# A gated S5/FFN kernel on one core: the first two pairs of w1 tiles in halves of 256 tokens, and the first loads spread over three queues

## The chip, the cores and the metric

One core of a Trainium2 chip runs the whole program. The metric is device time in microseconds (us); lower is better. Three runs of the kernel before gave 141.84, 142.42 and 142.87 us, median 142.42. Engines are named as in the profile: PE (TensorE matmul), PEld (its weight loads), DVE (VectorE), ACT (ScalarE), POOL (GpSimd), SP (SyncE, which here only issues transfers).

## The reference

For `x` of 2048 tokens by 448 features (bf16) the kernel computes a gated mix of a state-space layer `a` and a feed-forward layer `b`:

```python
g = sigmoid((x * gate_w).sum(-1, keepdims=True))
# a: complex diagonal recurrence, 448 states
dt = exp(log_dt); Lam_bar = exp(dt * Lam)
B_bar = ((Lam_bar - 1.0) / Lam)[:, None] * Bmat      # Bmat = B_re + 1j*B_im
Bu = einsum("bld,pd->blp", x, B_bar)
h_t = Lam_bar * h_{t-1} + Bu_t
a = 2.0 * einsum("blp,dp->bld", h, Cmat).real + x * Dskip
# b: 448 -> 1792 -> 448
b = silu(x @ w1) @ w2
out = g * a + (1 - g) * b
```

## The kernel before

**Tiling.** Tokens are cut into four chunks of 512 (`CH`). `x` is loaded token-major into `xnat` and transposed on PE into `xT` (features on partitions, in four blocks of up to 128). Each product tile is 128 output rows by 512 tokens and contracts 448 features as seven steps of 64 rows; two tiles make a *pair*, whose steps run side by side, one in the upper and one in the lower 64 rows of the PE array (L670). A pair has two halves: h=0 with four steps, h=1 with three. "F" tiles are rows of `x @ w1` (14 per chunk), evicted by ACT with Silu into `aT` (L641); "B" tiles are `x @ B` (7 per chunk), evicted into `UG` (L647 on DVE for the first chunk, L649 on ACT later). Then come the second feed-forward product (L775), the state rotation and scans on DVE (L705, L737), and the read-out with C (L796, `ot` L799, stores L802).

**What sets the order.** Every operation is entered in a `Plan` with an estimated cost and a priority; `order()` lists them by estimated time. PE is in order: its instructions run as they were entered. Loads are operations of the queue that issues them (`load`, L387 to L390): SP, ACT or POOL, each in the order that the plan gives. `Waits` then puts in semaphore waits; a flag `own` on a PE operation makes it wait also for earlier PE results in the same PSUM bank.

**The start, where the change is.**

- Warm-up: `NWARM` = 6 matmuls of 128x512 and one of 256 columns on constants (L463, L464), then the transposes of the first chunk of `x` (`x0_transposes`, L478; evictions L486 on DVE and L488 on ACT), then two fill matmuls (L499).
- `x` of the first chunk comes in two halves of 256 tokens (224 KB each): the first on SP's queue, the second on ACT's, both as the first issue of their queue. All 32 transposes are done before the first product.
- `w1` is cut into column groups (`w1cuts`, L392): W0 to W3 of 256 columns each (two F tiles each, one pair), and W4 of 768 columns. Each group is issued as its first 384 rows (192 KB, W4: 576 KB) and its last 128 rows (64 KB, W4: 192 KB); W0 goes as 128 KB on SP and two pieces of 64 KB on ACT.
- SP's order: x (first half), W0 (128 KB), three parameter rows (0.9 KB each), W1, W2, W3, then matrix B in four pieces, then W4, two broadcast rows (`gwb`, `dkb`), the next chunk of x, w2, C, and the last two chunks of x. The pieces of B, called B1 to B4 below, are A_B_re rows 0 to 383 (B1, 336 KB), A_B_re's last 64 rows (B2, 56 KB), A_B_im's last 64 rows (B3, 56 KB) and A_B_im rows 0 to 383 (B4, 336 KB). They land in tile `H`.
- POOL starts with constants (L443 to L456; the last that matters here is `SG`, L454), then waits for the parameters: `prmT` transposes them on PE (L543), DVE copies them to `pc` (L547), POOL takes a power (`dtc`, L550), and from there DVE makes phase tables (L551 to L569) and ACT sines and cosines (L567, L570).
- `x_products` enters the products. Pair 0 is W0's two tiles, pair 1 W1's, pair 2 W2's, pair 3 W3's. Its PE order is: pair 0 h=0, prmT, pair 1 h=0, pair 0 h=1, pair 2 h=0, pair 1 h=1, pair 3 h=0, then the transposes of B1 (24, L611, evictions L619 and L621), pair 2 h=1, the transposes of B2 to B4 (32, L611), then the first pair of B tiles and so on. All of this is in one in-order list, so a late operand holds up everything behind it.

Of the kernel before, what the change touches and what calls it, by code (L numbers as in the profile page):

```python
# [17 lines left out]
CH = 512  # L18
# [2 lines left out]
NFB = F_FF // 128  # L21
NSLOT = 7
NOT = 5
NWARM = 6
NFILL = 2
XCOL = [0, 128, 256, 320]

# [4 lines left out]
PE_MM = {512: 0.2157, 448: 0.1891, 128: 0.0560}  # L32
# [244 lines left out]
def bass_gated_mix__ssm_conv_s5__dense_activation_silu__prompt_kernel(nc, A_x, A_Lambda_re, A_Lambda_im, A_B_re, A_B_im, A_C_re, A_C_im,  # L277
               A_log_dt, A_Dskip, B_x, B_w1, B_w2, gate_w, out):
    with ExitStack() as ctx:
# [6 lines left out]
        x2, out2 = A_x[0], out[0]  # L286

        xnat = sb("xnat", [128, NTB, D_MOD], BF16)
        xT = sb("xT", [128, 4, S_TOK], BF16)
# [24 lines left out]
        ident = sb("ident", [128, 128], BF16)  # L314
# [8 lines left out]
        prm = sb("prm", [3, 512], BF16)  # L323
# [8 lines left out]
        SG = sb("SG", [128, 2, 4], F32)  # L332
# [25 lines left out]
        def bk(t, k=0):  # L358
            return ps[:, t.bank + k, :]
# [7 lines left out]
        def act_cost(n, aps=0):  # L367
            return 0.17 + n * 0.000833 + 0.09 * aps
# [4 lines left out]
        def ACT(fn, r, w, cost, prio, tag=""):  # L373
            return P.add("act", fn, r, w, cost, prio, tag=tag)

        def DVE(fn, r, w, cost, prio, tag=""):
            return P.add("dve", fn, r, w, cost, prio, tag=tag)

        def POOL(fn, r, w, cost, prio=10, tag=""):
            return P.add("pool", fn, r, w, cost, prio, tag=tag)  # L380

        def PE(fn, r, w, cost, tag=""):
            return P.add("pe", fn, r, w, cost, 0, tag=tag)
# [3 lines left out]
        def load(q, dst, src, name, nbytes, prio=None, after=()):  # L387
            nl[0] += 1
            prio = nl[0] if prio is None else prio
            P.add(q, lambda e: e.dma_start(dst, src), list(after), name.split(), 0.6 if q == "pool" else 0.5, prio, sem(), nbytes, tag="ld " + name)  # L390
# [3 lines left out]
        def load_w1(q, k, a, b):  # L394

            cols = slice(w1cuts[k], w1cuts[k + 1])
            src = B_w1[320:448, cols] if a == 3 else B_w1[128 * a:128 * b, cols].rearrange("(b p) f -> p b f", p=128)
            load(q, w1s[:, 3, cols] if a == 3 else w1s[:, a:b, cols], src, " ".join(f"w1_{k}_{i}" for i in range(a, b)),
                 256 * (b - a) * (cols.stop - cols.start))

        for h, q in enumerate(("sp", "act")):
            load(q, xnat[:, 2 * h:2 * h + 2, :], x2[256 * h:256 * h + 256, :].rearrange("(b p) d -> p b d", p=128), f"xn0{h}", 256 * 896)
        load_w1("sp", 0, 0, 2)
        load_w1("act", 0, 2, 3)
        load_w1("act", 0, 3, 4)
        for k, v in enumerate((A_log_dt, A_Lambda_re, A_Lambda_im)):
            load("sp", prm[k:k + 1, 0:448], v.rearrange("(o n) -> o n", o=1), f"prm{k}", 896)
        for k in range(1, len(w1cuts) - 2):
            load_w1("sp", k, 0, 3)
            load_w1("sp", k, 3, 4)  # L410
        Bnat = H[3][:, :, 0:D_MOD]
        load("sp", Bnat[:, 0:3, :], A_B_re[0:384, :].rearrange("(b p) d -> p b d", p=128), "H3_0 H3_1 H3_2", 384 * 896)
        load("sp", Bnat[0:64, 3, :], A_B_re[384:448, :], "H3_3", 64 * 896)
        load("sp", Bnat[64:128, 3, :], A_B_im[384:448, :], "H3_3i", 64 * 896)
        load("sp", Bnat[:, 4:7, :], A_B_im[0:384, :].rearrange("(b p) d -> p b d", p=128), "H3_4 H3_5 H3_6", 384 * 896)
        btn = {s: [f"BT{s}_{h}" for h in range(2)] for s in range(7)}
        load_w1("sp", len(w1cuts) - 2, 0, 3)
        load_w1("sp", len(w1cuts) - 2, 3, 4)
# [35 lines left out]
        POOL(lambda e: e.tensor_single_scalar(SG[:, 1, 3:4], sgn[:, :], -1.0, ALU.mult), ["SG", "sgn"], ["SG"], 0.2, 2)  # L454
        POOL(lambda e: e.memset(hpi[:, :], HALFPI), [], ["hpi"], 0.1, 2)
        POOL(lambda e: e.memset(eul[:, :], math.e), [], ["eul"], 0.1, 0)  # L456
        ACT(lambda e: e.preload_act_table_set("silu_and_others"), [], ["tbl"], 1.3, 9.5)

        tkz = Ps()
# [8 lines left out]
        def x0_transposes(q0, part, who):  # L468

            tk = Ps(2)  # L470

            def mm(pe):
                for q in (q0, q0 + 1):
                    for k in range(2):
                        o = ((q - q0) * 2 + k) * 64
                        for h in range(2):
                            p = slice(64 * h, 64 * h + 64)
                            r = pe.transpose(bk(tk, h).bitcast(BF16)[:, o:o + 64], xnat[p, 2 * part + k, XCOL[q]:XCOL[q] + 128], ident[p, p])  # L478
                return r
            PE(mm, [f"xn0{part}", "ident"], [tk], 4 * 0.054, "xT0")  # L480
            for h in range(2):
                src = lambda h=h: bk(tk, h).bitcast(BF16)[:, 0:256].rearrange("p (q b n) -> p q b n", q=2, n=64)
                dst = xT[:, q0:q0 + 2, 256 * part:256 * part + 256].rearrange("p q (b h n) -> p q b h n", h=2, n=64)[:, :, :, h, :]
                names = [f"xT0_{q}{part}{h}" for q in (q0, q0 + 1)]
                if who[h] == "d":
                    DVE(lambda e, src=src, dst=dst: e.tensor_copy(dst, src()), [tk], names, 0.28, 0, "xTe")  # L486
                else:
                    ACT(lambda e, src=src, dst=dst: e.activation(dst, src(), AF.Copy), [tk], names, act_cost(256), 0, "xTe")  # L488

        x0_transposes(0, 0, "da")  # L490
        x0_transposes(0, 1, "da")
        x0_transposes(2, 0, "da")
        x0_transposes(2, 1, "dd")

        tkw = Ps()

# [3 lines left out]
            return r  # L500
        PE(fill, [], [tkw], NFILL * 0.11, "fill")
        xn_of = {tc: {q: [f"xT{tc}_{h}" for h in range(2)] for q in range(4)} for tc in range(1, NCH)}
        xn_of[0] = {q: [f"xT0_{q}{part}{h}" for part in range(2) for h in range(2)] for q in range(4)}

        def x_transposes(tc, who):

# [29 lines left out]
        def parameters():  # L536

            prmn = [f"prm{k}" for k in range(3)]
            tkp = Ps()

            def prm_t(pe):
                for b in range(4):
                    r = pe.matmul(bk(tkp)[:, 4 * b:4 * b + 3], prm[0:3, 128 * b:128 * b + 128], ident[0:3, 0:3], start=True, stop=True)  # L543
                return r
            DVE(lambda e: e.tensor_copy(prm[:, 448:512], prm[:, 384:448]), prmn + ["xT0_211"], ["prm4"], 0.17, 0)
            PE(prm_t, prmn + ["prm4", "ident"], [tkp], 0.5, "prmT")
            DVE(lambda e: e.tensor_copy(  # L547
                pc[:, 0:3, :], bk(tkp)[:, 0:16].rearrange("p (b k) -> p k b", k=4)[:, 0:3, :]), [tkp], ["pc"], 0.2, 0)
            LDT, LRE, LIM = (pc[:, k, :] for k in range(3))
# [73 lines left out]
        def w1n(fb, i):  # L623
            return [f"w1_{q}_{i}" for q in range(len(w1cuts) - 1) if w1cuts[q] <= fb * 128 < w1cuts[q + 1]]

        def weights(tile, p0, p1, i):
            kind, tc, k = tile
            return w1s[p0:p1, i, k * 128:k * 128 + 128] if kind == "F" else BT[p0:p1, i, LCOL[k]:LCOL[k] + 128]
# [25 lines left out]
        def x_products(tiles, fill={}, wait=()):  # L654

            part = (list(zip([(i, 64) for i in (0, 1, 2, 3)], [(i, 0) for i in (0, 1, 3, 2)])),  # L660
                    list(zip([(i, 0) for i in (0, 1, 2)], [(i, 64) for i in (0, 1, 3)])))
            pairs = [tiles[t:t + 2] for t in range(0, len(tiles), 2)]
            toks = [Ps(2) for _ in pairs]

            def steps(k, h, a, z):
                def body(pe):
                    for n, cut in list(enumerate(part[h]))[a:z]:
                        for b, ((i, p0), tile) in enumerate(zip(cut, pairs[k])):
                            tc = tile[1]
                            r = pe.matmul(bk(toks[k], b), weights(tile, p0, p0 + 64, i), xT[p0:p0 + 64, i, tc * CH:(tc + 1) * CH],  # L670
                                          start=(h == 0 and n == 0), stop=(h == 1 and n == 2))
                    return r
                reads = [n for cut in part[h][a:z] for (i, _), tile in zip(cut, pairs[k])
                         for n in xn_of[tile[1]][i] + (w1n(tile[2], i) if tile[0] == "F" else btn[tile[2]])]
                return PE(body, list(dict.fromkeys(reads)), [toks[k]], (z - a) * PE_MM[512], f"{pairs[k][0][0]}{pairs[k][0][1]}")

            def half(k, h):
                if h == 0 and pairs[k][0] == ("F", 0, 0):
                    steps(k, 0, 0, 2)
                    steps(k, 0, 2, 4)  # L680
                else:
                    steps(k, h, 0, len(part[h])).own = h == 1
                if h:
                    evict(pairs[k], toks[k])

            half(0, 0)
            for f in fill.get(-1, ()):
                f()
            for k in range(len(pairs)):
                order = [lambda: half(k, 1)] + [lambda: half(k + 1, 0)] * (k + 1 < len(pairs))  # L690
                for n, f in enumerate(order if k - 1 in wait else order[::-1]):
                    f()
                    for m in fill.get((k, n), ()):
                        m()
                for f in fill.get(k, ()):
                    f()
# [223 lines left out]
```

## Time and profile before

| what | value |
|---|---|
| median of three runs | 142.42 us (141.84 to 142.87) |
| the profiled execution's own time | 142.07 us |
| its span in the profile | 140.2 us |
| DVE busy | 123.2 us (88%) |
| ACT busy | 89.0 us (63%) |
| POOL busy | 38.7 us (28%) |

The profile shows one execution. "L670" is line 670 of the kernel. A group of instructions is given with its line, its engine, what it writes and reads (`out<-in`), its shape and how often it ran. The chain of waits that ended last lists, in order of time, start, length and the work that the end of the program hangs on. A timeline gives start, length, engine, line and, in brackets, how long the engine was idle before and what ended that; "<-issue" means that nothing that the profile shows did. SPq, ACTq and POOLq are issues of transfers: their length is the issue, not the transfer, and the time to landing stands in the list of DMA issues. A table by windows gives each engine's busy time and the busy share of the 16 DMA engines in a stretch.

### The profile page before, as it was taken

How to read it: one execution, taken by the hardware profiler on the slowest of the kernel's cores; microseconds unless marked ns; L12 is line 12 of the kernel's file. 1: busy time of each engine (PE TensorE's matmuls, PEld its weight loads, DVE VectorE, ACT ScalarE, POOL GpSimd, SP SyncE). 2: the span in 40 equal slices, each digit the busy share in tenths (PEclk: the TensorE clock that was granted, in tenths of full speed). 3: DMA queues.
4: the chain of work that ended last, by engine and by line, in shares of the span. 5: the costliest groups of instructions: out<-in, count | busy, mean ns of one | idle time of the engine just before them, and what ended most of it. 6: DMA issues, size and time to landing. Idle time of an engine off the chain costs nothing.

```text
span 140.2 us, 3002 instructions
## 1 busy us (share of the span) xinstructions
PE 136.7 (97%) x1199; PEld 67.5 (48%) x1199; DVE 123.2 (88%) x179; ACT 89.0 (63%) x155; POOL 38.7 (28%) x72
## 2 busy tenths in 40 slices
PE   7999999999999999999999999999999999999992
PEld 2445554445544544455554544444455555555561
DVE  0369999999999999999999999999699999599153
ACT  3239758999998998713971886899920068412300
POOL 7160004201545600229560002833000204222220
PEclk9999999999999999999999999999999999999999
DMA  4988999820447730108975000947001402245342
GB/s 142 262 254 251 320 380 271 201 55 0 69 78 123 126 45 0 37 0 127 158 142 139 0 5 0 134 92 115 2 2 57 106 0 37 33 98 120 46 94 70
DMA packets 18500, 14.71 MB, mean 105 GB/s; under 512 B 2867, under 2 KB 18358, under 8 KB 18486
## 3 DMA queue, kind: packets, MB, share of 16 engines
q0 software_dynamic: 6064, 5.51, 24.7%
q1 hardware_dynamic: 11862, 8.65, 20.4%
q10 hardware_dynamic: 560, 0.36, 0.8%
q8 instruction: 9, 0.15, 0.5%
q14 instruction: 5, 0.04, 0.1%
HBM read 7.17 MB, written 1.84 MB: 64 GB/s over the span
## 4 chain that ended last, share of the span: by engine, by line
PE 97%; DVE 0%; issue 0%
PE ps L670 46%; PE ps L775 31%; PE ps L796 15%; PE ps L463 2%; PE ps L515 1%; PE ps L478 1%; PE ps L815 1%; PE ps L611 1%; PE ps L499 0%; DVE ot L799 0%; PE ps L464 0%; PE ps L543 0%
## 5 line engine op out<-in xcount | busy, mean ns | idle before, releaser
L670 PE MATMUL ps<-xT,w1s 64*128 64x512 bf16 x392 | 48.6, 380 | 0.0
L775 PE MATMUL ps<-w2s,aT 128*128 128x448 bf16 x224 | 43.4, 353 | 0.0
L641 ACT ACTIVATE aT<-ps 128x1024 bf16<-128x1024 f32 (+1 forms) x30 | 28.7, 970 | 10.8 <-PE ps L670 10.6
L775 PEld LDWEIGHTS ps<-w2s,aT 128*128 128x128 bf16 x224 | 21.6, 98 | 20.7 <-issue 0.8
L670 PEld LDWEIGHTS ps<-xT,w1s 64*128 64x128 bf16 x392 | 20.0, 95 | 22.7 <-issue 1.2
L670 PE MATMUL ps<-xT,BT 64*128 64x512 bf16 x196 | 25.8, 376 | 0.0
L783 POOL DMA_DIRECT2D xnat<-fe x16 | 13.9, 889 | 38.1 <-ACT fe L781 35.7
L781 ACT ACTIVATE fe<-ps,g 128x448 bf16<-128x448 f32 x16 | 10.1, 633 | 21.8 <-PE ps L775 17.8
L390 POOL DMA_DIRECT2D UG<-Gf x27 | 15.1, 566 | 30.4 <-DVE Gf L737 30.0
L737 DVE TENSOR_TENSOR_SCAN Gf<-rc,gin,H 128x512 f32<-128x512 f32 x14 | 17.0, 1268 | 0.0
L796 PE MATMUL ps<-CP,H 128*128 128x448 bf16 (+2 forms) x98 | 16.4, 326 | 0.0
L670 PEld LDWEIGHTS ps<-xT,BT 64*128 64x128 bf16 x196 | 11.1, 94 | 10.8
L799 DVE SCALAR_TENSOR_TENSOR ot<-ps,g,xnat 128x448 bf16<-128x448 f32 (+2 forms) x18 | 10.8, 626 | 4.6 <-issue 3.3
L705 DVE TENSOR_TENSOR H<-UG,COS 128x3584 bf16<-128x3584 bf16 (+4 forms) x10 | 12.7, 1272 | 0.0
L796 PEld LDWEIGHTS ps<-CP,H 128*128 128x128 bf16 x98 | 8.9, 98 | 7.5 <-issue 0.4
L649 ACT ACTIVATE UG<-ps 128x1024 bf16<-128x1024 f32 (+1 forms) x12 | 10.7, 916 | 1.8 <-PE ps L670 1.8
L705 DVE TENSOR_TENSOR PO<-UG,SIN 128x1536 bf16<-128x1536 bf16 (+1 forms) x8 | 8.7, 1091 | 2.9 <-ACT UG L747 1.5
L390 POOL DMA_DIRECT2D UG<-UG x8 | 4.6, 580 | 23.0 <-ACT UG L649 11.6
L850 ACT ACTIVATE xnat<-xnat,g 128x448 bf16<-128x448 bf16 x16 | 10.0, 665 | 0.2
L843 ACT ACTIVATE junk<-xg 128x448 bf16<-128x448 bf16 x16 | 9.2, 573 | 0.2
L705 DVE TENSOR_TENSOR PI<-UG,SIN 128x512 bf16<-128x512 bf16 (+2 forms) x13 | 9.2, 730 | 0.0
L737 DVE TENSOR_TENSOR_SCAN Gf<-rc,gin,H2C 128x512 f32<-128x512 f32 x7 | 8.5, 1269 | 0.0
(102 smaller groups left out, 124.9 us busy)
## 6 DMA issues: line engine op xcount, KB each, us to landing
UG<-Gf POOLq DMA_DIRECT2D x21, 128.0 KB, 2.4
xnat<-fe POOLq DMA_DIRECT2D x16, 112.0 KB, 2.8
out_dram<-ot SPq DMA_DIRECT2D x15, 112.0 KB, 1.7
w2s<-in_B_w_dram SPq DMA_DIRECT2D x1, 1568.0 KB, 11.6
xnat<-in_A_x_dram SPq DMA_DIRECT2D x3, 448.0 KB, 7.6
w1s<-in_B_w_dram SPq DMA_DIRECT2D x4, 192.0 KB, 3.4
w1s<-in_B_w_dram SPq DMA_DIRECT2D x1, 576.0 KB, 6.4
UG<-UG POOLq DMA_DIRECT2D x8, 64.0 KB, 2.3
```

The lines of the kernel that those rows point to most:

```text
L390: P.add(q, lambda e: e.dma_start(dst, src), list(after), name.split(), 0.6 if q == "pool" else 0.5, prio, sem(), nbytes, tag="ld " + name)
L641: ACT(lambda e, src=src, dst=dst: e.activation(dst, src(), AF.Silu), [tk, "tbl"], [f"aT{tc % 2}_{m}" for m in names], act_cost(512 * n), 2 ...
L649: ACT(lambda e, src=src, dst=dst: e.activation(dst, src(), AF.Copy), [tk], [f"{un}{m}" for m in names], act_cost(512 * n), 5, "U")
L670: r = pe.matmul(bk(toks[k], b), weights(tile, p0, p0 + 64, i), xT[p0:p0 + 64, i, tc * CH:(tc + 1) * CH], start=(h == 0 and n == 0), stop=( ...
L705: DVE(lambda e: e.tensor_tensor(o, a, b, op), r, w, dve_cost(n, 2), prio, tag)
L737: DVE(lambda e, s=s, b=b, init=init: e.tensor_tensor_scan(Gf[:, s, :], rc[:, b:b + 1].to_broadcast([128, CH]), A[:, s, :], init, ALU.mult, ...
L775: r = pe.matmul(bk(tk)[:, 0:D_MOD], aT[tc % 2][:, fb, o:o + 128], w2s[:, fb, :], start=(fb == 0), stop=(fb == NFB - 1))
L781: ACT(lambda e: e.activation(f[:, :], bk(tk)[:, 0:D_MOD], AF.Copy, scale=g1[:, tb:tb + 1]), [tk, f"g1_{tc}"], [fn], act_cost(448, 1), 7, "fe")
L783: P.add("pool", lambda e: e.dma_start(Tb[:, tb, :], f[:, :], accum_op=ALU.add), [fn, f"Tb{tb}"], [f"Tb{tb}"], 0.94, 2, sem(), 115000, tag= ...
L796: r = pe.matmul(bk(tk)[:, 0:b - a], H[tc][:, s, o:o + 128], CP[:, s, a:b], start=(s == 0), stop=(s == NSLOT - 1))
L799: DVE(lambda e, tk=tk, a=a, b=b: e.scalar_tensor_tensor(ot[tb % NOT][:, a:b], bk(tk)[:, 0:b - a], g[:, tb:tb + 1], Tb[:, tb, a:b], ALU.mul ...
L850: ACT(lambda e, tb=tb: e.activation(Tb[:, tb, :], xnat[:, tb, :], AF.Copy, scale=g[:, tb:tb + 1]), [f"xd{tc}", f"g_{tc}"], [f"Tb{tb}"], ac ...
```

## The change

1. **Warm-up.** `NWARM` goes from 6 to 5.
2. **Queues.** SP issues x's first half, the three parameter rows, x's second half, W1, W2, W3, W4 and the rest as before. ACT issues all of W0 (128, 64 and 64 KB), no x. POOL issues B1 to B4, in this order, after `SG` (L454 before) and ahead of `dtc`.
3. **Transposes.** The 32 transposes of x's first chunk are split: 16 for its first half of tokens ahead of the first product, 16 for its second half after prmT. Their evictions are DVE and ACT in turn throughout; DVE's copy of the parameters comes ahead of the second two.
4. **Products.** Pairs 0 and 1 are done in halves of 256 tokens (`of`): 56 matmuls of 256 columns instead of 28 of 512. The new PE order up to pair 3 is: pair 0 h=0 (first tokens), prmT, transposes of the second tokens, pair 0 h=1 (first), pair 1 h=0 (first), pair 0 h=1 (second), pair 1 h=1 (first), pair 0 h=0 (second), pair 1 h=1 (second), pair 2 h=0 (all tokens), pair 1 h=0 (second), pair 3 h=0, transposes of B1, pair 2 h=1, transposes of B2 to B4. From pair 3 on nothing is reordered on PE.

```diff
-NWARM = 6
+NWARM = 5
...
-        for h, q in enumerate(("sp", "act")):
-            load(q, xnat[:, 2 * h:2 * h + 2, :], x2[256 * h:256 * h + 256, :].rearrange("(b p) d -> p b d", p=128), f"xn0{h}", 256 * 896)
-        load_w1("sp", 0, 0, 2)
+        def load_x0(h):
+            load("sp", xnat[:, 2 * h:2 * h + 2, :], x2[256 * h:256 * h + 256, :].rearrange("(b p) d -> p b d", p=128), f"xn0{h}", 256 * 896)
+
+        load_x0(0)
+        load_w1("act", 0, 0, 2)
         load_w1("act", 0, 2, 3)
         load_w1("act", 0, 3, 4)
         for k, v in enumerate((A_log_dt, A_Lambda_re, A_Lambda_im)):
             load("sp", prm[k:k + 1, 0:448], v.rearrange("(o n) -> o n", o=1), f"prm{k}", 896)
+        load_x0(1)
...
-        load("sp", Bnat[:, 0:3, :], A_B_re[0:384, :].rearrange("(b p) d -> p b d", p=128), "H3_0 H3_1 H3_2", 384 * 896)
-        load("sp", Bnat[0:64, 3, :], A_B_re[384:448, :], "H3_3", 64 * 896)
-        load("sp", Bnat[64:128, 3, :], A_B_im[384:448, :], "H3_3i", 64 * 896)
-        load("sp", Bnat[:, 4:7, :], A_B_im[0:384, :].rearrange("(b p) d -> p b d", p=128), "H3_4 H3_5 H3_6", 384 * 896)
...
+        load("pool", Bnat[:, 0:3, :], A_B_re[0:384, :].rearrange("(b p) d -> p b d", p=128), "H3_0 H3_1 H3_2", 384 * 896, -1, ["SG"])
+        load("pool", Bnat[0:64, 3, :], A_B_re[384:448, :], "H3_3", 64 * 896, -1, ["SG"])
+        load("pool", Bnat[64:128, 3, :], A_B_im[384:448, :], "H3_3i", 64 * 896, -1, ["SG"])
+        load("pool", Bnat[:, 4:7, :], A_B_im[0:384, :].rearrange("(b p) d -> p b d", p=128), "H3_4 H3_5 H3_6", 384 * 896, -1, ["SG"])
...
         x0_transposes(0, 0, "da")
-        x0_transposes(0, 1, "da")
         x0_transposes(2, 0, "da")
-        x0_transposes(2, 1, "dd")
...
-            DVE(lambda e: e.tensor_copy(prm[:, 448:512], prm[:, 384:448]), prmn + ["xT0_211"], ["prm4"], 0.17, 0)
-            PE(prm_t, prmn + ["prm4", "ident"], [tkp], 0.5, "prmT")
+            DVE(lambda e: e.tensor_copy(prm[:, 448:512], prm[:, 384:448]), prmn + ["xT0_200"], ["prm4"], 0.17, 0)
+            PE(prm_t, prmn + ["prm4", "ident"], [tkp], 0.27, "prmT")
...
-            def steps(k, h, a, z):
+            def steps(k, h, a, z, of=(0, 1)):
+                t0, t1 = 256 * of[0], 256 * of[-1] + 256
                 def body(pe):
                     for n, cut in list(enumerate(part[h]))[a:z]:
                         for b, ((i, p0), tile) in enumerate(zip(cut, pairs[k])):
-                            tc = tile[1]
-                            r = pe.matmul(bk(toks[k], b), weights(tile, p0, p0 + 64, i), xT[p0:p0 + 64, i, tc * CH:(tc + 1) * CH],
-                                          start=(h == 0 and n == 0), stop=(h == 1 and n == 2))
+                            o = tile[1] * CH
+                            r = pe.matmul(bk(toks[k], b)[:, t0:t1], weights(tile, p0, p0 + 64, i), xT[p0:p0 + 64, i, o + t0:o + t1],
+                                          start=(h == of[0] and n == 0),
+                                          stop=(h != of[0] and n == len(part[h]) - 1))
                     return r
...
+            def begin():
+                steps(0, 0, 0, 2, (0,))
+                steps(0, 0, 2, 4, (0,))
+                for f in fill.get(-1, ()):
+                    f()
+                x0_transposes(0, 1, "da")
+                x0_transposes(2, 1, "da")
+                steps(0, 1, 0, 3, (0,)).own = True
+                steps(1, 0, 0, 4, (0,))
+                steps(0, 1, 0, 3, (1,))
+                steps(1, 1, 0, 3, (0,)).own = True
+                steps(0, 0, 0, 4, (1,)).own = True
+                evict(pairs[0], toks[0])
+                steps(1, 1, 0, 3, (1,))
+                half(2, 0)
+                steps(1, 0, 0, 4, (1,)).own = True
+                evict(pairs[1], toks[1])
```

More of the change, by code (lines that the diff above doesn't have):

```diff
@@ L502, in bass_gated_mix__ssm_conv_s5__dense_activation_silu__prompt_kernel @@
         xn_of = {tc: {q: [f"xT{tc}_{h}" for h in range(2)] for q in range(4)} for tc in range(1, NCH)}
-        xn_of[0] = {q: [f"xT0_{q}{part}{h}" for part in range(2) for h in range(2)] for q in range(4)}
         def x_transposes(tc, who):
@@ L672, in body @@
                     return r
                 reads = [n for cut in part[h][a:z] for (i, _), tile in zip(cut, pairs[k])
-                         for n in xn_of[tile[1]][i] + (w1n(tile[2], i) if tile[0] == "F" else btn[tile[2]])]
-                return PE(body, list(dict.fromkeys(reads)), [toks[k]], (z - a) * PE_MM[512], f"{pairs[k][0][0]}{pairs[k][0][1]}")
+                         for n in ([f"xT0_{i}{t}{u}" for t in of for u in range(2)] if tile[1] == 0 else xn_of[tile[1]][i])
+                         + (w1n(tile[2], i) if tile[0] == "F" else btn[tile[2]])]
@@ L677, in half @@
+                return PE(body, list(dict.fromkeys(reads)), [toks[k]], (z - a) * PE_MM[512] * len(of) / 2, f"{pairs[k][0][0]}{pairs[k][0][1]}")
             def half(k, h):
[L678 to L682, printed above, removed]
+                steps(k, h, 0, len(part[h])).own = h == 1
                 if h:
                     evict(pairs[k], toks[k])
-            half(0, 0)
@@ L687, in x_products @@
-            for f in fill.get(-1, ()):
-                f()
-            for k in range(len(pairs)):
+            def begin():
[15 more added lines that the diff above has]
+                evict(pairs[1], toks[1])
@@ L690, in x_products @@
+            k0 = 0
+            if pairs[0][0] == ("F", 0, 0):
+                begin()
+                k0 = 2
+            else:
+                half(0, 0)
+            for k in range(k0, len(pairs)):
                 order = [lambda: half(k, 1)] + [lambda: half(k + 1, 0)] * (k + 1 < len(pairs))
```

## The prediction, made before the changed kernel ran

> **What bounds the kernel now.** I read the page's busy times first, then the chain of waits that ended last, then the timeline of the first 16 us with the DMA issues.
>
> ```profile
> PE 136.7 (97%) x1199; PEld 67.5 (48%) x1199; DVE 123.2 (88%) x179; ACT 89.0 (63%) x155; POOL 38.7 (28%) x72
> ```
>
> ```profile
> 0.76 2.72 PE ps L463 x6
> ...
> 3.70 1.12 PE ps L478 x29
> 4.82 0.54 PE ps L499 x2
> 5.36 1.59 PE ps L670 x7
> ...
> 7.13 3.99 PE ps L670 x36
> 11.13 0.35 PE ps L611 x24
> 11.48 0.65 PE ps L670 x6
> 12.12 0.52 PE ps L611 x32
> 12.64 7.57 PE ps L670 x70
> ```
>
> The chain is PE from 0.76 us to the end, each piece starting where the last ended: PE is the bound, and a reordering of the same PE work gains nothing by itself. Only PE work removed, PE work moved out of the slow start, or a new PE wait can move the end. The slow start shows in the eight products at 5.29 us (four pairs in 1.66 us, 0.415 a pair) beside the 36 after 7.07 us (18 pairs in 4.06, 0.226).
>
> ```profile
> 4.13 0.21 POOL L454 TENSOR_SCALAR SG<-sgn 128x1 f32<-128x1 f32 x1
> 5.67 1.00 SPq L390 DMA_DIRECT2D H<-in_A_B_re_dram  x2
> 6.71 1.22 SPq L390 DMA_DIRECT2D H<-in_A_B_im_dram  x2
> 7.43 1.05 POOL L550 TENSOR_TENSOR dtc<-eul,pc 128x4 f32<-128x4 f32 x1 [3.09 <-DVE pc L547]
> 7.98 1.02 SPq L390 DMA_DIRECT2D w1s<-in_B_w_dram  x2
> 11.97 0.55 PEld L611 LDWEIGHTS ps<-ident,H 64*128 64x128 bf16 x32 [0.34 <-issue]
> ```
>
> ```profile
> w1s<-in_B_w_dram SPq DMA_DIRECT2D x1, 576.0 KB, 6.4
> H<-in_A_B_im_dram SPq DMA_DIRECT2D x1, 336.0 KB, 4.6
> ```
>
> To see here: B4 is the second of the two B_im issues, at about 7.35 us, and lands 4.6 us later, at 11.9; PE loads it at 11.97. B4 arrives just in time, with no slack. W4's first piece (576 KB) is issued behind it, at 7.98, and lands at 14.4; its second at 14.8.
>
> **The change part by part**, against the profiled execution (142.07 us; span 140.2 and 1.9 around it; 0.35 under the median of the runs).
>
> *Warm-up and first transposes.* One matmul less is 2.72/6 = 0.45 us. The transposes at 3.70 then start when x's first half has landed: 0.72 + 2.9 = 3.6 now, while 224 KB of the second half share the engines; afterwards 128 KB of W0 do. Bounds for their start: 3.26 (end of the warm-up) and 3.70; I take 3.45. That moves 0.25 us of work into the slow stretch, where a pair costs 0.415 instead of 0.226, so it is worth 0.13 at the end; with the wait on the second half gone from between the transposes I take -0.15, bounds -0.25 and 0.
>
> *Products by halves.* 28 matmuls of 512 columns become 56 of 256: the same columns, 28 more weight loads of 94 ns. A 256-column pair needs 0.11 us of PE; the B1 transposes, each pair with its own two loads, run 12 pairs in 0.35 us, 0.03 a pair, so the loads hide behind the matmuls. Price: 0; if half of the loads showed, 14 x 0.094 = 1.3, taken as the far bound. The two further waits on PE's own results have three pairs (0.33 us) between writer and reader; a product lasts 0.376 us and the next starts 0.216 after it, so 0.16 has to be covered, and is. Nothing else queues on PE for them.
>
> *Second transposes and parameters.* 16 transposes, before and after: 0. They come at about 5.7 us; x's second half is issued at about 2.2 on SP, behind the first half and the parameters, and lands with the rest of what has landed by 5.3 now (W0's last piece: 1.76 + 3.6). Cover 0.4; without it PE would wait some 0.5. The parameters land earlier (SP issues them at 1.2 instead of 1.72), so `pc` comes about 1.2 us sooner, at 6.1.
>
> *B on POOL.* Removes four issues (2.22 us) from SP and puts them on POOL, behind L454, which ends at 4.34. Prices there: 0.52 us (a 64-row copy at 27.16) to 0.91 (the accumulating `fe` copy). B4's issue starts at 4.34 + 3 x 0.52 = 5.9 to 4.34 + 3 x 0.91 = 7.1, and POOL is free at 6.4 to 8.0. `dtc`, now queued behind B, starts in those bounds instead of 7.43, and with it DVE's tables. DVE is nearly full from 8.5 us, so 0.6 late would stay; but its last state work ends at 130.3 and PE reads it at 131.8, a cover of 1.5. Price 0; with the cover gone, up to 0.6.
>
> *W4 moves up.* SP has nothing between W3 and W4 any more, so W4 is issued 2.3 us earlier, at 5.67 and 6.2, and the rows behind it too. B4, at 5.9 to 7.1, is issued behind W4's first piece. This is the step that decides. What do the rows say of a POOL transfer issued into a loaded DMA?
>
> ```profile
> 17.52 1.66 SPq L390 DMA_DIRECT2D xnat<-in_A_x_dram  x2
> 21.26 1.48 POOL L390 DMA_DIRECT2D UG<-UG  x2 [11.41 <-DVE UG L647]
> ```
>
> ```profile
> UG<-UG POOLq DMA_DIRECT2D x2, 64.0 KB, 5.0
> ```
>
> The two 64 KB copies issued at 21.26 landed after 5.0 us in the median, the like pair issued at 27.16 after 2.4. The x loads that SP issued at 17.52 took 7.7, to 25 to 26 us; the copies landed at 26 to 27. So a POOL transfer is served behind what SP has already issued, not ahead of it. Then B4 and W4's first piece change places: B4 lands when that piece lands now, 14.4. The extra queue can use DMA time that is idle now: busy share 0.78 from 5.0 to 6.6 us and 0.88 from 6.6 to 8.4, of which B can reach some 0.3. I take 14.1, bounds 11.9 (as now) and 17.9 (behind dkb and the next x, 10.27 + 7.6, should POOL's issues be slow). The bytes agree: 285 GB/s x 3.5 us + 215 x 2.9 moves 1.62 MB between 8.4 and 14.8, B and W4 are 1.59 MB.
>
> PE reaches the 32 transposes at 12.0 - 0.15 = 11.85 and waits until 14.15. All behind it on PE (first B pair and everything after) is 2.15 later than now, for the chain has no later gap to give it back; DVE and ACT wait with it. The first gain vanishes in this wait. W4, first used behind the first B pairs, is early and gains nothing.
>
> Sum: 142.07 + (14.15 - 12.00) = 144.2; on the median 144.6. I forecast 144.4.
>
> **Rivals.**
>
> *Turns (R).* If the DMA engines took POOL's and SP's descriptors in turn, B would share with W2 and W3 from about 5.7 us: 512 KB of those finish after 1024 KB, at 220 KB/us by 10.35, landing 10.65 against 9.85 when PE wants W3 (10.09 now): 0.8 late. B's remaining 270 KB then share with W4: 540 KB at 250 is 12.5, landed 12.8, wanted at 12.65. Net +0.8 by bytes, +1.8 if it goes by descriptors (W's 512 bytes for B's 896), where W3 itself comes last at 11.7; middle +1.3, so 143.5. For it: POOL's queue is separate (q0 beside q1). Against it: the 5.0 us above. The Trainium skill, DMA: Bandwidth & Descriptors, "Queues, rings and completion order", says that each DMA engine goes round the rows it has work for, a packet at a time; by that rule this rival would be the forecast, and the row of 5.0 us disagrees with it.
>
> *Hidden (H), the other side.* B4 lands by 12.0, because POOL's early start (4.34 against 5.67) outweighs W4's. Then only the first part counts: 142.1 to 142.4, not slower. The point from which it decides: B4 no more than 0.1 us later than now. For it: idle DMA share at 5 to 8 us. Against: B4 is issued behind W4's 576 KB.
>
> *Issue (P).* POOL takes over 1 us for a piece of 384 rows; B4 falls behind the next x, up to 17.9: up to 148, about 147.
>
> *Clock (F).* The slow start ends sooner: at 3.7 instead of about 7 it would save 3.3 x (1 - 0.226/0.415) = 1.5 us, about 140.9. Nothing in the rows says that one warm-up matmul less does this. The Trainium skill, TensorE: Matmul & The Clock Gate, Part 1, lets the clock rise after a busy window of about 3.4 us that runs free of the kernel's start; by that an execution could fall either way, whatever the change.
>
> **How the numbers follow.** Arrival order (A, 144.4) 0.45; R 0.22; H 0.20; P 0.08; F 0.05. "Within 1%" (1.42 us, about what a measurement of this kernel can tell from no change) is 141.0 to 143.84. Slower: nearly all of A (0.42), P (0.08), a third of R (0.08) = 0.58. Same: H, the rest of R and A: 0.37. Faster: 0.05. Range 142.0 to 145.6: it reaches to H, and leaves out P, F and a little of H. A alone: 143.6 to 145.2.
>
> **What would show it.** First transposes at 3.3 to 3.6; PE idle ahead of the 32 transposes of `H`, put down to a DMA, until about 14; B4's landing 7 to 8 us after its issue; W4 landed ahead of it; no gap later. R: the idle time stands ahead of pair 3's products (W3). H: no PE idle time before 13 us. I am wrong if POOL's transfers are served ahead of SP's, or if 256-column pairs take over 0.13 us.

## The result, and the profile after

| what | before | after |
|---|---|---|
| median | 142.27 us (141.81 to 142.87, 6 runs) | 144.50 us (143.75 to 144.88, 6 runs) |
| the profiled execution | 142.07 us, span 140.2 | 144.58 us, span 142.8 |

The changed kernel takes 1.0151 of the time before, with a 95% interval from 1.0112 to 1.019: 2.2 us slower. 144.4 was forecast. Here and below the ratios leave out executions more than 1.5% above the fastest of the same kernel, while the medians in us count them.

The page's busy line of the changed kernel answers to the one shown of before:

```profile
PE 137.5 (96%) x1226; PEld 69.5 (49%) x1226; DVE 122.9 (86%) x178; ACT 89.4 (63%) x156; POOL 41.2 (29%) x76
```

PE is busy 0.8 us longer (27 instructions more: 28 products and one warm-up matmul less), the span is 2.6 us longer, and DVE is not busier: the other 1.8 us are idle time of PE, and much of its work early on is slow. The chain of the changed kernel says where (start, length, what; the pieces up to 2.17 us, the issues of SP, are left out):

```profile
2.17 4.40 DMA xnat<-in_A_x_dram
...
6.61 0.61 PE ps L481 x14
7.22 5.38 PE ps L674 x60
12.60 0.35 PE ps L611 x24
12.95 0.65 PE ps L674 x6
13.60 0.94 issue
14.54 0.64 PE ps L611 x32
15.18 7.55 PE ps L674 x70
```

Read it beside the chain of before. The 24 transposes of B1 start at 12.60 instead of 11.13, so 1.47 us are lost before PE comes to B at all. Then PE, which had no gap before, stands 0.94 us ahead of the 32 transposes; their start has moved from 12.12 to 14.54 (from 12.00 to 14.54 by the timeline, where PE's first start counts). The later pieces are as long as before, to a few hundredths. The last piece of PE ends at 140.03 instead of 137.51, so the 2.5 us in hand at 14.54 are the 2.5 us at the end.

The end of PE's wait is B4. These are the lines of POOL and of the weight loads in the timeline, and two lines of the list of transfers (KB, us from issue to landing):

```profile
4.65 1.59 POOL L390 DMA_DIRECT2D H<-in_A_B_re_dram  x2 [0.31 <-POOL SG L453]
6.22 1.32 POOL L390 DMA_DIRECT2D H<-in_A_B_im_dram  x2
7.53 1.10 POOL L550 TENSOR_TENSOR dtc<-eul,pc 128x4 f32<-128x4 f32 x1
14.51 0.55 PEld L611 LDWEIGHTS ps<-ident,H 64*128 64x128 bf16 x32 [1.41 <-issue]
```

```profile
H<-in_A_B_im_dram POOLq DMA_DIRECT2D x1, 336.0 KB, 7.7
w1s<-in_B_w_dram SPq DMA_DIRECT2D x1, 576.0 KB, 7.6
```

B4 is issued at 6.74 and lands 7.7 us later, at 14.45; PE's weights start at 14.51. W4's first piece, issued at 5.66, is down at 13.3. "<-issue" in brackets is not an engine that was slow: nothing on an engine releases that wait, and the landing fits it to 0.1 us.

### The profile page after: what moved, and what is told of

Same layout as the page of the kernel before. It is cut to its first block, busy times and chain, and to the rows that moved or that the text cites. A ratio compares the mean times of both kernels' runs of the same rounds, so it can differ in the third digit from the quotient of the medians.

```text
span 142.8 us, 3056 instructions
## 1 busy us (share of the span) xinstructions
PE 137.5 (96%) x1226; PEld 69.5 (49%) x1226; DVE 122.9 (86%) x178; ACT 89.4 (63%) x156; POOL 41.2 (29%) x76
## 4 chain that ended last, share of the span: by engine, by line
PE 93%; DMA 3%; issue 1%; SPq 1%; DVE 0%
PE ps L674 45%; PE ps L799 30%; PE ps L820 15%; DMA xnat<-in_A_x_dram 3%; PE ps L515 1%; SPq L390 1%; PE ps L839 1%; PE ps L611 1%; PE ps L481 0%; DVE ot L823 0%
## 5 line engine op out<-in xcount | busy, mean ns | idle before, releaser
L674 PE MATMUL ps<-xT,w1s 64*128 64x512 bf16 (+1 forms) x420 | 49.7, 371 | 0.0
L674 PEld LDWEIGHTS ps<-xT,w1s 64*128 64x128 bf16 x420 | 21.8, 96 | 22.4 <-issue 1.1
L823 DVE SCALAR_TENSOR_TENSOR ot<-ps,g,xnat 128x448 bf16<-128x448 f32 (+2 forms) x18 | 10.8, 626 | 7.5 <-issue 6.2
L674 PEld LDWEIGHTS ps<-xT,BT 64*128 64x128 bf16 x196 | 11.4, 94 | 10.3
L649 ACT ACTIVATE UG<-ps 128x1024 bf16<-128x1024 f32 (+1 forms) x12 | 10.8, 921 | 1.8 <-PE ps L674 1.8
## 6 DMA issues: line engine op xcount, KB each, us to landing
w2s<-in_B_w_dram SPq DMA_DIRECT2D x1, 1568.0 KB, 12.4
```

Source lines behind the costliest of these rows:

```text
L674: r = pe.matmul(bk(toks[k], b)[:, t0:t1], weights(tile, p0, p0 + 64, i), xT[p0:p0 + 64, i, o + t0:o + t1], start=(h == of[0] and n == 0), ...
L823: DVE(lambda e, tk=tk, a=a, b=b: e.scalar_tensor_tensor(ot[tb % NOT][:, a:b], bk(tk)[:, 0:b - a], g[:, tb:tb + 1], Tb[:, tb, a:b], ALU.mul ...
```

## The experiments

Theory A is the forecast's: B4's late landing sets the end. Theory S says that the start does it: x's second half, the idle pieces of PE and the slow stretch of the products. After the first four runs S was made sharper as theory C: idle pieces early in the kernel put off the moment from which PE runs at full speed. Its rival D has the halved products themselves, or chance, in their place. Twelve kernels ran, each beside the kernel before, and ratios are to that.

### B back on SP

The changed kernel, with all four pieces of B issued by SP again, between W3 and W4.

```diff
-        load("pool", Bnat[:, 0:3, :], ...
+        load("sp", Bnat[:, 0:3, :], ...
```

> The changed kernel with the four loads of B back on SP's queue between W3 and W4; all else as changed. Theory A (the prediction's: B4's late landing sets the end, the start gains 0.15): the wait ahead of the 32 transposes goes and the time is about 142.1. Theory S (start: PE is already 1.46 late at B1's transposes, 12.42 against 10.96, because x's second half lands at 6.57 and the slow stretch lasts longer, and B4 adds the rest): the start's loss stays, B4 lands at about 12, time about 143.7 and no idle time ahead of the 32 transposes.

144.46 us, ratio 1.013 (1.0089 to 1.017): no better than the changed kernel. B4 landed at 12.1 and PE did not wait for it, so the wait was gone and the time stayed. The chain of this kernel shows what took its place:

```profile
6.98 6.17 PE ps L674 x64
...
14.15 0.47 PE ps L611 x32
14.62 0.10 issue
14.72 7.73 PE ps L674 x70
```

The piece of 70 products starts at 14.72, against 12.64 before: 2.1 us late with no wait for B. (The last piece of PE there is 2.7 us late; the other 0.6 come at 106 to 116 us, where PE waits for work of DVE and ACT.) Many of the 64 products ahead of it run slowly. The groups of PE from 8.2 to 8.9 us have this line (mean ns at the end of the busy part):

```profile
L674 PE MATMUL ps<-xT,w1s 64*128 64x256 bf16 x10 | 1.3, 417 | 0.0
```

At full speed the same product takes 269 ns (shown below). So undoing one cause alone gained nothing, for another lay under it.

### B on POOL alone

The kernel before, with B1 to B4 on POOL behind `SG` and nothing else changed.

```diff
-        load("sp", Bnat[:, 0:3, :], ...
+        load("pool", Bnat[:, 0:3, :], ..., -1, ["SG"])
```

> The kernel before with only B's four loads moved to POOL behind SG; products, transposes, warm-up and the other queues as before. Theory A (B4 falls behind W4 and alone sets the end): B4 lands at 14 to 14.5, PE idles about 2 us ahead of the 32 transposes, time 144.3 to 144.8, the whole loss of the change. Theory S (start and B4 share the loss): the same wait, since B4's landing does not depend on PE, so the same end; a time under 143.2 would say that B4's lateness came from the changed first loads. The rival of turns: PE also waits ahead of pair 3 (W3 landing after 10).

144.8 us, ratio 1.0136 (1.0099 to 1.0173). B on POOL, without halves, costs as much as the whole change. But the wait is not where the forecast put it. PE's timeline:

```profile
11.91 1.89 PE L670 MATMUL ps<-xT,w1s 64*128 64x512 bf16 x8 [2.41 <-DMA w1s<-in_B_w_dram]
13.57 0.87 PE L611 MATMUL ps<-ident,H 64*128 64x64 bf16 x24
```

PE stands 2.41 us for W3, not for B. W3's tail (its 64 KB) was issued by SP at 5.14 and landed at 11.77, 6.6 us later; in the kernel before it landed at 8.5. POOL's B1 was served meanwhile: between 7.0 and 11.8 us the queue q0 (POOL's) moved 183 packets beside 816 of SP's q1 (packets, MB, share of the 16 engines' time).

```profile
q1 hardware_dynamic: 816, 0.88, 54.3%
q0 software_dynamic: 183, 0.57, 37.6%
```

After the wait eight products of 512 columns take 1.89 us, where the same eight take 1.04 at full speed; the table by windows has PE's granted clock at 0.50 from 12.4 to 14.4 us. In this execution the wait was followed by a fall of the clock. It does not make the loss: in the other five timed executions the mean granted clock is 0.999 or 1.0, and they took 144.2 to 145.2 us.

### Halves alone

The changed kernel, with every load back on the queue that it had before (B too).

```diff
-        load_x0(0)
-        load_w1("act", 0, 0, 2)
+        for h, q in enumerate(("sp", "act")):
+            load(q, xnat[:, 2 * h:2 * h + 2, :], ...)
+        load_w1("sp", 0, 0, 2)
...
```

> The changed kernel with all queues as in the kernel before (x's second half first on ACT, W0's 128 KB and parameters on SP, B on SP); five warm-up matmuls, split transposes and products by halves stay. Theory A: 142.1, the small gain of the start. Theory S: no wait for x's second half, since it is first on ACT's queue and lands at about 4; if the queue order made the start late the time is 142.0 to 142.4, if the halves or the shorter warm-up made the slow stretch longer it is 143.0 or more, and products of 417 ns instead of 269 ns last to about 9 us.

143.74 us, ratio 1.0078 (1.0047 to 1.0109). All of x was down at 3.8 us, yet the piece of products after the 32 transposes started at 14.35. The products took some 416 ns each until about 10.3 us. A smaller part is on ACT, in the chain:

```profile
22.13 0.60 ACT aT L638
22.72 0.61 ACT COS L567
23.33 0.92 ACT xT L522
```

The eviction of the next chunk's `xT` now stands behind a cosine in ACT's list, where before it came right behind the eviction of `aT`. So the halves, the split transposes and the five warm-up matmuls together cost about 1 us without any queue moved. (The profiled execution took 144.47 us, 0.7 more than the median.)

### W4 held back until B4 has landed

The changed kernel; `late` names B4's landing for W4 and for all that SP issues behind it.

```diff
-            P.add(q, lambda e: e.dma_start(dst, src), list(after), ...)
+            P.add(q, lambda e: e.dma_start(dst, src), list(after) + late, ...)
```

> The changed kernel in which W4 and all loads behind it on SP's queue wait until B4 has landed, so that B competes with W3 alone. Theory A (W4 overtakes B4): B4 lands by 11.5 to 12, no idle time ahead of the 32 transposes; the end then is set by the start's 1.46 us, 143.5 to 143.8, or by a later wait for W4 (landing about 16) or the next x. Rival (a POOL transfer is slow in itself): B4 still lands after 13.5, and the time stays at 144.5 or more.

144.06 us, ratio 1.0102 (1.0069 to 1.0135). The interval overlaps that of the changed kernel, so the time alone tells little, but the transfer answers clearly. Issued at 6.74 as in the changed kernel, B4 now needs 5.0 us instead of 7.7:

```profile
H<-in_A_B_im_dram POOLq DMA_DIRECT2D x1, 336.0 KB, 5.0
```

It lands at 11.8, and PE has no wait at the 32 transposes, which start at 13.30. So W4, and what SP issues behind it, is what makes B4 late. W3's tail still landed at 10.8, against 8.5 before. The gain is paid back 20 us later, where C comes late because SP's queue stood still (PE's waits):

```profile
PE ps L841 <- DMA H2C<-in_A_C_re_dram: 1.4, 1, 1.4
```

### One warm-up matmul less, alone

The kernel before, with:

```diff
-NWARM = 6
+NWARM = 5
```

> The kernel before with the warm-up cut from six matmuls to five and nothing else; one 0.42 us of PE work less, so PE should now stand idle for about 0.4 us ahead of the first transposes, until x has landed at 3.6 us. Theory C (an idle PE ahead of the rise puts the rise of the clock off, and that is what the halves and the new queues cost at the start): the products run slowly until 8 to 10.5 us instead of 6.6 (5.1 in the run with B on POOL), two to four us longer at 0.45 us lost for each, so 1.0 to 1.6 us slower, 143.6 to 144.3 beside a before of 142.6. Rival D (the slow stretch depends on the halved products themselves, or varies by itself, and the warm-up is only filler): within 0.3 us of before, 142.3 to 142.9, with the slow products ending at 5 to 7.5 us.

142.48 us, ratio 1.0002 (0.9979 to 1.0026): no difference, as rival D has it. The idle piece was only 0.22 us, and this execution's products were at full speed from the first (eight in 1.04 us from 4.81). So the warm-up does not cost anything by itself. PE's timeline shows what an early start is worth here:

```profile
10.38 0.81 PE L670 MATMUL ps<-xT,w1s 64*128 64x512 bf16 x6
12.08 0.64 PE L611 MATMUL ps<-ident,H 64*128 64x64 bf16 x32 [0.89 <-issue]
```

PE came a microsecond early and waited 0.89 for B4, which landed at 11.98. The kernel before has this limit too.

### Three kernels meant to have no idle piece

```diff
-NWARM = 5
+NWARM = 6
...
-            DVE(lambda e: e.tensor_copy(prm[:, 448:512], ...), prmn + ["xT0_200"], ...)
+            DVE(lambda e: e.tensor_copy(prm[:, 448:512], ...), prmn + ["xT0_210"], ...)
...
-                for f in fill.get(-1, ()):
-                    f()
                 x0_transposes(0, 1, "da")
                 x0_transposes(2, 1, "da")
+                for f in fill.get(-1, ()):
+                    f()
```

This edit was made to the halves alone, to the changed kernel with B on SP, and to the changed kernel; in the last two x's second half was also put ahead of the parameter rows.

> Halves alone (all loads as before), but with six warm-up matmuls and the parameter transposes behind the second transposes of x, so that PE has no idle piece before the products. Theory C: the clock rises as early as before (5 to 7.5 us) and the loss of 1.0 us that the halves alone had is gone, 142.3 to 142.9. Rival D (halved products cost by themselves, by their 28 more weight loads or by their two waits): the loss stays, 143.4 to 144.1, and the 256-column products at full clock last longer than half of the 512-column ones.

> The changed kernel with B back on SP, x's second half ahead of the parameter rows, six warm-up matmuls and the parameter transposes behind the second transposes. Theory C: no idle piece of PE before the rise, so the products are at full clock by 7.5 us and the time is 142.3 to 143.0, 1.5 us less than the same kernel with the idle pieces (144.46). Rival D: the early idle pieces are not the cause, so 144.0 to 144.8 again.

> As the run beside it, but B stays on POOL as in the changed kernel. Theory C with B's late landing as a second, overlapping cause: the start gains about 1.5 us over the changed kernel, but W3 at 9.4 to 11.8 and B4 at about 14.4 us stop PE in its place, so 144.0 to 144.6, and 1.2 to 2.0 us slower than the run beside it. If B's place on POOL costs nothing (as the run with B back on SP, which gained nothing, could be read), both runs agree within 0.4 us.

144.7 us (1.0158, 1.0121 to 1.0195), 144.44 us (1.0125, 1.0086 to 1.0164) and 146.11 us (1.0215, 1.0171 to 1.0259). The numbers missed, and so did the edit: it made the idle piece larger. The DVE copy ahead of the parameter transposes had moved behind DVE's evictions of the second transposes, and PE stood for it in all three. PE's timeline of the second of them:

```profile
5.20 0.39 PE L674 MATMUL ps<-xT,w1s 64*128 64x256 bf16 x4 [0.32 <-DMA w1s<-in_B_w_dram]
5.42 0.41 PE L481 MATMUL ps<-ident,xnat 64*128 64x64 bf16 x16
6.69 0.23 PE L543 MATMUL ps<-ident,prm 3*128 3x3 bf16 x4 [0.86 <-DVE prm L545]
6.86 6.19 PE L674 MATMUL ps<-xT,w1s 64*128 64x256 bf16 x64
```

Its 16 transposes at 5.42 run in 0.41 us, so PE was at full speed; the 64 products behind the wait take 6.19 us, so it no longer was. The table by windows shows the granted clock falling (its clock records begin only when the clock first rises, and until then the table prints 1.00; the columns behind the window are PE, PEld, DVE, ACT and POOL busy, then PEclk, DMA share and GB/s):

```profile
4.40:6.40 2.00, 1.03 (x25) 0.68 (x24) 0.60 (x4) 0.91 (x3) 0.00 (x0) 1.00 0.84 234
6.40:8.40 2.00, 1.71 (x22) 1.33 (x24) 0.68 (x5) 0.02 (x1) 1.10 (x2) 0.68 0.90 258
8.40:10.40 2.00, 2.00 (x22) 1.46 (x20) 1.90 (x10) 0.00 (x0) 1.16 (x2) 0.50 0.91 256
```

The third of the three has the same wait (0.87 us) and the same 6.19 us. But the fall is not what the medians cost: one step of 3.41 us at half clock takes 0.012 off the mean granted clock of an execution, and only two of six executions of each of the two kernels show a mean as low (0.986 to 0.988). The one profiled here took 145.67 us, 1.2 more than its kernel's median.

The edit also reordered DVE's list for the first 20 us. In the first of the three, PE was at full speed by 7.5 us, its products ended 0.8 us later than before, and the rest of its loss came late, among waits for DVE and ACT (the longest 1.0 us, L796 for `ot`). For theory C these three decide nothing, but for one thing. In the first of them 64 products take 4.52 us from 7.45 on, and they hold 48 halves and 16 whole ones, as much as 40 whole ones: 4.36 us of starts / 40 = 0.109 each. Before, 36 whole ones take 3.89 / 36 = 0.108. Halved products cost nothing at full speed in this trace.

Moving x's second half did what it should: issued at 1.21, ahead of the parameter rows, it landed after 3.7 us, at 4.9, where the changed kernel has 4.4 us and 6.57.

### The sixth warm-up matmul back, and nothing moved

```diff
-NWARM = 5
+NWARM = 6
...
-        PE(warm, [], [tkz], NWARM * 0.43 + 0.21, "warm")
+        PE(warm, [], [tkz], 5 * 0.43 + 0.21, "warm")
```

Made to the same three kernels: the halves alone, the changed kernel with B on SP, and the changed kernel itself. The plan is still told the cost of five, so that every other instruction of every engine keeps its order.

> Halves alone (all loads as before) with the sixth warm-up matmul back and nothing else moved: the first transposes then start at 3.7 us instead of 3.5 and the two idle pieces of PE (0.25 and 0.14 us) close. Theory C, mended (the rise of the clock is put off when idle pieces fall among the thin work ahead of it; halved products cost nothing at full clock): the products are at full clock by 7.6 us and the loss of 1.0 us of the halves alone goes down to 0.0 to 0.5, 142.5 to 143.0 beside a before of 142.5. Rival D (the halved order itself puts the rise off or costs time): 143.4 to 144.0, with the rise again at 9 to 10.5 us.

> The changed kernel with B back on SP and six warm-up matmuls, nothing else moved. In the run with five the idle pieces were 0.43 and 0.25 us and the clock rose at 10.6 us; with six the first is filled and the data of the second has landed. Theory C: rise by 7.6 us, the first B products at 12.5 to 13.0 us instead of 14.6, time 142.5 to 143.3. Rival D: 144.0 to 144.8 again.

> The changed kernel itself with six warm-up matmuls. Theory A on record with the prediction (B4, from POOL, is the last to come and sets the end whatever happens ahead of it): B4 at 14.3 to 14.6 us again, PE waits there 1 to 2 us, 144.0 to 144.6, and 1.2 us or more slower than the same with B on SP. If the slow clock alone makes the loss: as the run with B on SP, 142.5 to 143.3.

| | five warm-ups | six warm-ups |
|---|---|---|
| halves alone | 1.0078 (1.0047 to 1.0109) | 1.0063 (1.0036 to 1.0089), 143.46 us |
| all of the change but B | 1.0130 (1.0089 to 1.0170) | 1.0043 (1.0014 to 1.0071), 143.09 us |
| the whole change | 1.0151 (1.0112 to 1.0190) | 1.0179 (1.0133 to 1.0224), 144.85 us |

The middle row is the answer for theory C. The idle piece of 0.42 us at 3.3 us is closed; PE's timelines have it with five warm-ups and not with six:

```profile
3.69 0.61 PE L481 MATMUL ps<-ident,xnat 64*128 64x64 bf16 x16 [0.42 <-DMA xnat<-in_A_x_dram]
3.66 0.61 PE L481 MATMUL ps<-ident,xnat 64*128 64x64 bf16 x16
```

With it 0.0087 x 142.5 = 1.2 us come back; the two intervals do not overlap. The chain of the kernel with six:

```profile
7.05 4.20 PE ps L674 x58
...
12.24 0.47 PE ps L611 x32
12.71 0.10 issue
12.81 7.73 PE ps L674 x70
```

Its groups from 8.2 to 8.9 us have the same kind of products as above, at full speed:

```profile
L674 PE MATMUL ps<-xT,w1s 64*128 64x256 bf16 x17 | 1.1, 269 | 0.0
```

The traces' clock records, which begin when PE's clock first rises to full, show the same in all kernels with halved products: with five warm-ups the rise comes at 8.96, 9.29, 10.28 and 10.60 us (four kernels), with six at 3.56 to 6.54 (six kernels). In the kernel before it comes at 6.59. One matmul less is not enough by itself: with whole products and five warm-ups it came at 4.36, although that kernel too has an idle piece (0.22 us).

With B on SP and six warm-ups some 0.6 us of the loss stay (0.0043 x 142.5); their cause stays open.

The last row is the answer for theory A. With the same early start but B on POOL, nothing is gained, and B's place costs 1.0179 - 1.0043 = 0.0136, or 1.9 us. PE's timeline of that kernel has both waits:

```profile
7.12 3.33 PE L674 MATMUL ps<-xT,w1s 64*128 64x256 bf16 x50 [0.24 <-DMA w1s<-in_B_w_dram]
11.85 1.04 PE L674 MATMUL ps<-xT,w1s 64*128 64x512 bf16 x8 [1.40 <-DMA w1s<-in_B_w_dram]
12.71 0.53 PE L611 MATMUL ps<-ident,H 64*128 64x64 bf16 x24
13.06 0.83 PE L674 MATMUL ps<-xT,w1s 64*128 64x512 bf16 x6
15.62 0.56 PE L611 MATMUL ps<-ident,H 64*128 64x64 bf16 x27 [1.73 <-issue]
```

W3's tail lands at 11.71 and B4 at 15.53, 1 us later than the 14.3 to 14.6 that was expected. What PE gains ahead of them turns into waiting for them.

The first row missed: 142.5 to 143.0 was expected. Its products were at full speed by 5.5 us, but B4 landed at 12.55 in that execution, 0.6 us later than before, and PE waited 0.97 for it; the cosine ahead of `xT` on ACT took another 0.5. That the idle pieces cost the halves alone anything is not shown.

### W3's tail on ACT's queue

The kernel before, with:

```diff
-            load_w1("sp", k, 3, 4)
+            load_w1("act" if k == 3 else "sp", k, 3, 4)
```

> The kernel before, with W3's 64 KB tail issued by ACT behind its table load (about 3.5 us) instead of by SP, so that B1 to B4 are issued 0.5 us sooner. If B4's landing is what the start of the kernel before waits for (it was the last to come by 0.1 us, and with an early rise of the clock PE stood 0.9 us for it), B4 lands 0.1 to 0.5 us sooner: 142.0 to 142.5 beside 142.5. If the DMA engines are already full there: B4 again at 11.9 to 12.0 and no difference.

142.06 us, ratio 0.9968 (0.9944 to 0.9992): 0.4 us faster than the kernel before, by an interval that ends just under 1. ACT issued the tail at 2.29, SP issued B4 at 6.88 instead of 7.35, and it landed at 11.24 instead of 11.9. The chain has the 32 transposes 0.3 us earlier than before and no wait ahead of them:

```profile
11.81 0.47 PE ps L611 x32
12.27 7.62 PE ps L670 x70
```

That B4 makes the gain is not shown. In this trace PE is 0.3 us ahead before it comes to B: its first eight products took 1.37 us instead of 1.66. What the earlier B4 did there is to be down when PE came for it, at 11.64; at 11.9 it would have cost that lead.

## Why the prediction was right, point by point

**The end, and what sets it: right.** The forecast let PE wait at the 32 transposes for B4 until 14.15; they start at 14.54, 0.4 late, and the end is 2.5 us later where 2.15 was forecast. B4's issue fell inside its bounds (5.9 to 7.1: 6.74). Holding W4 back brought B4 to 11.8, so the step that the earlier place of W4 (and of what follows it on SP) delays B4 is shown. Nothing later gave the time back.

**How the transfers share: the rule was wrong, though its landing time was near.** "A POOL transfer is served behind what SP has already issued" held for B4 and W4's first piece, but not for B1 and W3. W3's tail, issued by SP at 5.14, while POOL was still issuing B1, landed at 11.43, 3 us later than before; in the same time, 7.0 to 11.4 us, POOL's queue moved 0.47 MB of the changed kernel's traffic:

```profile
q1 hardware_dynamic: 1006, 0.95, 71.4%
q0 software_dynamic: 158, 0.47, 30.0%
```

The queues were served side by side. That is rival R, whose count by descriptors had W3 last at 11.7; the runs gave 11.43, 11.71 and 11.77. R missed that B4 comes as late as A says. That 14.1 came so near 14.45 is in part luck, since the rule behind it has W3 undisturbed; in three other kernels with B on POOL and W4 right behind W3, B4 landed at 14.40, 14.67 and 15.53. The Trainium skill, DMA: Bandwidth & Descriptors, "Queues, rings and completion order", has each DMA engine go round its queues a packet at a time; W3's three landings agree with it in that the queues take turns. How much goes in a turn the traces leave open: from 8 to 11 us of the changed kernel, with transfers of both queues outstanding, 594 packets of SP's queue moved and 114 of POOL's. The 5.0 us of the two small copies was no evidence against turns: from 22.5 to 26 us of the kernel before, 63 packets of POOL's queue moved beside 1061 of SP's.

**The first transposes: failed, at no cost.** -0.15 was taken for a start at 3.45. They started at 3.68, for x's first half landed hardly earlier (3.63 instead of 3.66) with 128 KB of W0 beside it in place of 224 KB of x.

**x's second half: the step failed.** "Lands with the rest of what has landed by 5.3" left a cover of 0.4. It landed at 6.57, and PE stood 0.42 us for it. The landing was read from bytes alone; three loads of one row were ahead of it on the queue, and issued ahead of them it came at 4.9.

**The slow stretch: not in the sum.** The forecast had PE at the transposes at 11.85; it came at 13.60. Of these 1.75 us, 0.42 are the wait for x's second half. Some 1.2 belong, by the middle row of the table, to the missing warm-up matmul, which left an idle piece when x did not come earlier. An estimate from the clock agrees: full speed began at 8.96 instead of 6.59 us, and 2.4 x (1 - 0.226/0.415) is 1.1. "One warm-up matmul less" was priced as 0.45 us of work gone; alone it is worth nothing (1.0002), with the halves and the new first loads, B on SP, it cost 1.2 us. Rival F looked for this effect on the other side only, as a gain. In the changed kernel this late start is hidden under the wait for B4, and so the forecast came out right without it: PE was late by 1.75 us, and then waited 0.94 where 2.3 had been forecast. That this step did no harm to the number is luck: for the kernel with B back on SP the same sum gives 142.1, and 144.46 was measured.

**Halves and `dtc`: right.** Halved products cost nothing at full speed (0.109 against 0.108, one trace). `pc` came at 6.24 (6.1 forecast), `dtc` started at 7.53 (6.4 to 8.0 forecast), and no later wait for DVE appears in the changed kernel's chain.

**Rival H fell** with the wait of 0.94 us, and P did not come about: of POOL's two issues of 384 rows one took 1.01 us, the other 0.81, and B4 did not fall behind the next x.

What stays open: how little PE has to do for its clock to stay down or fall, and whether the idle piece itself or the lesser work of PE puts off the rise; the halves alone (idle 0.25 us, rise at 10.28) and the one warm-up less alone (0.22 us, 4.36) hardly differ in it. Each kernel was profiled once, so the 1.2 us rest on the two timed ratios, and the mechanism on one trace each of four kernels with five warm-ups and six with six.

## What to carry to other kernels

Where two causes end at the same place on an in-order engine, undoing either one alone can gain nothing: take out both, and each one by one, before a cause is called harmless. More traffic is not an earlier operand: with B on POOL alone the core moved 4.28 MB in its first 16 us instead of 3.73, and W3 came 3 us later. A second queue changes who is served first, and what is delayed may be an operand of the queue that was not touched. Before shortening a warm-up, look at what arrives at its end: if the data comes no sooner, the time saved is an idle piece, and that may put off PE's full speed (1.2 us in one pair of kernels here, nothing that can be told in the others).

## What the runs showed of the hardware that was not expected

- **The clock can fall after short waits.** In the run with the wait of 0.86 us the trace's clock records have PE at full clock from 3.70, at 0.50 from 7.11 and at full again from 10.52; in the run with B alone on POOL, at 0.50 from 11.88 to 15.30, after a wait of 2.41 us. The steps are 3.41 us each. The Trainium skill, TensorE: Matmul & The Clock Gate, Part 1, gives a window of 3413 ns, and the steps agree with it. Idle time alone does not decide: the profiled execution of the changed kernel with six warm-up matmuls had idle pieces of 1.40 and of 1.73 us and kept its clock; another of its six, with a mean granted clock of 0.988, did not. Means of 0.986 to 0.988 show in nine timed executions of seven of the twelve kernels, and in none of 60 of the kernel before.
- **Traffic sags some 2 us behind the loads of one row.** The three parameter rows of 0.9 KB are issued between 1.2 and 2.1 us in the changed kernel and between 1.7 and 2.6 in the kernel before. The transfer rates of the first 16 us, in slices of 0.4 us, of the changed kernel and then of the kernel before:

```profile
GB/s 0 0 0 0 56 166 316 347 252 95 89 158 298 316 318 328 296 270 307 335 376 331 324 350 380 275 315 312 276 294 280 294 311 346 332 364 379 402 358 365
```

```profile
GB/s 0 0 0 0 76 159 363 376 343 337 315 339 195 152 228 234 274 256 180 196 304 311 247 208 272 298 313 272 324 311 229 235 242 223 151 220 192 262 329 352
```

The rate falls to 95, 89 and 158 GB/s from 3.6 to 4.8 us in the one, with x's second half issued and waiting, and to 195 and 152 from 4.8 to 5.6 in the other, 1.5 and 2.1 us behind the end of the last of these issues. That the rows are the cause was not tried; no kernel ran without them.
